# Transposes by the DMA crossbar instead of by TensorE in a sliding-window attention with a two-layer MLP

## The chip, the cores and the metric

The kernel runs on one core of a Trainium2 chip. The metric is the device time of one execution in microseconds (us). The profiler's span, from the first to the last instruction, is 1.7 to 1.9 us shorter than the device time of the same run. Engines are named as the profile names them: PE is TensorE (matmuls), PEld its weight loads, DVE is VectorE, ACT is ScalarE, POOL is GpSimd, SP is SyncE and SPq the queue in which SyncE issues DMAs.

## The reference

Attention over 4 batches of 8 heads, 768 positions, head size 64. Each query sees the 128 latest keys and 4 "sink" keys at the start of its sequence. The result, 3072 x 512, goes through a GEMM to 2048, an exact GELU and a GEMM back to 512.

```python
scores = scale * np.matmul(q, k.transpose(0, 1, 3, 2))
keep = is_sink | in_window            # 4 sinks, window 128
a = softmax(np.where(keep, scores, -1e9))
x = (a @ v).transpose(0, 2, 1, 3).reshape(B * S, H * D)
h = x @ w_in                          # 512 -> 2048
out = (0.5 * h * (1.0 + erf(h * inv_sqrt2))) @ w_out
```

## The kernel before

Queries are worked in 12 groups of 256 (g = 0 to 11), three to a batch, and two groups make a chunk (c = 0 to 5). For each chunk the kernel does the first GEMM (64 matmuls) and then the second (64 matmuls, in 16 slots of 4), and between the matmuls it prepares the attention of the next chunk. During the first GEMM it casts and transposes q and k of the next chunk; in the slots of the second it does scores, exponentials, the product with v (`av`) and the transposes of the result x. So the first GEMM of a chunk needs `xt` complete, which the slots before it produce.

All SyncE DMAs go through one queue, in program order. Loads use a ring of 10 staging tiles; `pump` issues every load whose staging tile the program has already freed.

```python
def casts(g, engs=(nc.vector, nc.vector, nc.vector)):
    for kind, eng in zip("qkv", engs):
        take(kind, g, eng)            # cast, marks the staging tile as free
    pump()                            # issues loads on nc.sync

def qk_transpose(g, pp, eng=nc.vector):
    pt = psB.tile([P, 2, 2, 2, P], BF16, name="qkps", tag="bank")
    # ... eight nc.tensor.transpose into pt
    copy(eng, qkt, pt)
    # ... for groups that begin a batch: 4 small GpSimd copies into SK (sink keys)

def x_transpose(g, p):                # one slot after av(g, p)
    # ... two nc.tensor.transpose into the bank of av
    nc.vector.tensor_copy(out=XT[c][:, p, o : o + Q2], in_=tp)

for c in range(NCH):
    side = {0: lambda: casts(ga), 1: lambda: qk_transpose(ga, 0), 2: lambda: qk_transpose(ga, 1),
            4: lambda: casts(gb), 5: lambda: qk_transpose(gb, 0), 6: lambda: qk_transpose(gb, 1)}
    for f2 in range(NFT // 2):
        gemm1(c, f2)
        if f2 in side:
            side[f2]()
    if c == 0:
        for j in range(8):
            take("wo", j, G_)         # casts of the second weight, on GpSimd
            pump()                    # ... and behind each, a load
    att = attention_slots(c + 1, 16) if nxt else [[] for _ in range(16)]
    for s in range(16):
        gemm2(c, s // 4, s % 4)
        for w in att[s]:
            w()
```

The softmax here doesn't subtract the row's maximum and nothing guards it: scores larger than these inputs give would overflow.

## Time and profile before

| | before |
|---|---|
| device time, median of 4 runs | 264.16 us |
| span of the profiled run | 261.3 us |
| PE busy | 88% of the span |
| DVE, ACT, POOL busy | 47%, 44%, 12% |
| first GEMM of chunk 0 begins | 31.8 us |
| length of chunks 0, 1, 2, 3, 4 | 42.9, 39.4, 38.5, 37.8, 39.4 us |
| chunk 5 and the end | 31.4 us |

Here and below a chunk lasts from the first matmul of its first GEMM to that of the next chunk, read from the order of time on PE. In chunks 1 to 4 PE is nearly always busy. Chunk 0 is longer: PE waits 3.3 us in it for casts of the second weight, which is still being loaded, and its granted clock stood at half until 35.0 us.

### The profile page before, as it was taken

What the parts mean: (1) busy time and instruction counts of PE and PEld (TensorE: products, weight loads), DVE (VectorE), ACT (ScalarE), POOL (GpSimd) and SP (SyncE); (2) the same over time, 40 slices, a digit from 0 to 9 for tenths busy, and PEclk for the clock granted to TensorE, in tenths of its full rate; (3) what the DMA queues carried; (4) which work ended last, traced back from release to release, by engine and by line L of the source; (5) the groups of instructions that cost most, each with busy time, mean ns of one, the idle gap of its engine ahead of it and who ended that gap; (6) DMA issues with size and microseconds to landing.
All of it is one profiled execution on the core that took longest, in us unless ns stands there. A gap on an engine that the chain in (4) does not pass through costs nothing.

```text
span 261.3 us, 4320 instructions
## 1 busy us (share of the span) xinstructions
PE 230.7 (88%) x1734; PEld 118.2 (45%) x1764; DVE 122.1 (47%) x277; ACT 115.4 (44%) x120; POOL 32.4 (12%) x82
## 2 busy tenths in 40 slices
PE   0467699869999989999999999999999989999994
PEld 0235445325445535444535444545445445544441
DVE  0284844247844256844346734357643267610111
ACT  0556336555315585314575325585135666136300
POOL 7177500690000000002000000200000000000000
PEclk9998589999999999999999999999999999999999
DMA  8999999999999991129920146001210010110022
GB/s 155 218 273 348 257 229 271 387 240 229 200 221 283 228 168 43 43 96 225 203 48 34 43 129 112 3 2 41 80 40 3 0 40 4 75 48 0 0 83 80
DMA packets 84756, 33.84 MB, mean 129 GB/s; under 512 B 75520, under 2 KB 79616, under 8 KB 84736
## 3 DMA queue, kind: packets, MB, share of 16 engines
q1 hardware_dynamic: 82656, 33.04, 54.8%
q10 hardware_dynamic: 2080, 0.52, 1.1%
q8 instruction: 14, 0.23, 0.4%
q14 instruction: 6, 0.05, 0.1%
HBM read 27.26 MB, written 6.29 MB: 128 GB/s over the span
## 4 chain that ended last, share of the span: by engine, by line
PE 58%; DMA 13%; DVE 8%; SPq 7%; ACT 7%; issue 5%; POOL 1%; another core or an unknown queue 0%; ACTq 0%; POOLq 0%; DVEq 0%
PE big L399 26%; PE po L418 21%; SPq L170 7%; ACT et L304 5%; DMA st<-in_moe_w_out_dram 5%; DMA st<-in_moe_w_in_dram 4%; DMA st<-in_v_dram 4%; PE qkps L244 3%; DVE osb L427 3%; PE big L295 2%; PE bank L383 2%; DVE x L368 1%; DVE et L315 1%; PE bank L356 1%; ACT gt L407 1%
## 5 line engine op out<-in xcount | busy, mean ns | idle before, releaser
L418 PE MATMUL po<-WOUT,gt 128*128 128x512 bf16 x365 | 91.5, 380 | 5.3 <-POOL WOUT L193 3.3
L399 PE MATMUL big<-xt,WIN 128*128 128x512 bf16 x373 | 88.0, 383 | 0.7 <-issue 0.2
L407 ACT ACTIVATE gt<-big 128x1024 bf16<-128x1024 f32 x48 | 49.1, 1023 | 88.4 <-PE big L399 87.2
L399 PEld LDWEIGHTS <-WIN 128*128 128x128 bf16 x384 | 37.0, 99 | 41.6 <-issue 2.4
L304 ACT ACTIVATE et<-big 128x1024 bf16<-128x1024 f32 (+1 forms) x48 | 44.5, 954 | 19.8 <-PE big L295 11.5
L418 PEld LDWEIGHTS <-gt 128*128 128x128 bf16 x384 | 33.1, 98 | 41.2 <-issue 10.9
L308 DVE TENSOR_TENSOR et<-et,mask 128x1024 bf16<-128x1024 bf16 x32 | 24.2, 758 | 28.7 <-ACT et L304 28.6
L427 DVE COPY osb<-po 128x512 f32<-128x512 f32 x24 | 16.5, 688 | 39.7 <-PE po L418 39.6
L193 DVE COPY qkt<-qkps 128x1024 bf16<-128x1024 bf16 x22 | 15.2, 691 | 35.3 <-PE qkps L244 35.3
L256 POOL COPY sk<-qkt 64x4 bf16<-64x4 bf16 x32 | 6.9, 215 | 129.0 <-DVE qkt L193 127.9
L244 PE MATMUL qkps<-ident,q 128*128 128x128 bf16 x96 | 13.2, 234 | 8.1 <-DVE q L193 7.9
L295 PE MATMUL big<-qkt 64*128 64x128 bf16 (+1 forms) x256 | 18.6, 249 | 2.0 <-ACT et L304 2.0
L368 DVE TENSOR_TENSOR x<-bank,rz 128x256 bf16<-128x256 f32 x44 | 18.7, 424 | 1.5
L356 PE MATMUL bank<-vo,et 128*128 128x65 bf16 x176 | 18.7, 198 | 0.2 <-POOL sk L256 0.2
L383 PE MATMUL bank<-ident,x 128*128 128x128 bf16 x88 | 12.9, 230 | 6.0 <-DVE x L368 5.9
L348 PE MATMUL bank<-vo,et 128*128 128x65 bf16 x148 | 17.2, 197 | 0.1
L383 PEld LDWEIGHTS <-x 128*128 128x128 bf16 x96 | 6.6, 101 | 22.5 <-DVE x L368 20.6
L356 PEld LDWEIGHTS <-et 128*128 128x128 bf16 x192 | 15.8, 103 | 2.0 <-issue 0.9
L348 PEld LDWEIGHTS <-et 128*128 128x128 bf16 x160 | 15.0, 103 | 0.9 <-DVE et L308 0.3
L244 PE MATMUL qkps<-ident,k 128*128 128x128 bf16 x96 | 13.2, 233 | 1.9 <-ACT k L191 1.9
L244 PEld LDWEIGHTS <-q 128*128 128x128 bf16 x96 | 8.9, 105 | 13.0 <-DVE q L193 7.9
L389 DVE COPY xt<-bank 128x256 bf16<-128x256 bf16 x44 | 12.5, 285 | 3.8 <-PE bank L383 3.8
(52 smaller groups left out, 146.5 us busy)
## 6 DMA issues: line engine op xcount, KB each, us to landing
st<-in_q_dram SPq DMA_DIRECT2D x24, 256.0 KB, 5.1
st<-in_v_dram SPq DMA_DIRECT2D x24, 256.0 KB, 4.9
out_dram<-osb SPq DMA_DIRECT2D x24, 256.0 KB, 2.0
st<-in_k_dram SPq DMA_DIRECT2D x22, 256.0 KB, 4.8
st<-in_moe_w_in_dram SPq DMA_DIRECT2D x8, 512.0 KB, 7.9
st<-in_moe_w_out_dram SPq DMA_DIRECT2D x8, 512.0 KB, 9.3
st<-in_k_dram ACTq DMA_DIRECT2D x2, 256.0 KB, 5.6
```

The costliest lines, as they stand in the source:

```text
L244: nc.tensor.transpose(pt[:, a, w, e, :], src[:, e, 2 * p : 2 * p + 2, :].rearrange("s h d -> s (h d)"), ident,)
L295: nc.tensor.matmul(ps[:, hl, c : c + n * P], lhsT=kb[r : r + D, :], rhs=qt(g, p)[r : r + D, e : e + n, :].rearrange("p e n -> p (e n)"), s ...
L304: nc.scalar.activation(out=et[:, :, c0:], in_=ps[:, :, c0:], func=AF.Exp, scale=att_scale)
L308: nc.vector.tensor_tensor(out=et.rearrange("p h (e n) -> p (h e) n", e=2), in0=et.rearrange("p h (e n) -> p (h e) n", e=2), in1=mask.unsqu ...
L348: nc.tensor.matmul(pov[:, e, hl, :], lhsT=et[:, hl, 2 * e * P : (2 * e + 1) * P], rhs=low[:, h, :], start=(i == 0), stop=False, skip_group ...
L356: nc.tensor.matmul(pov[:, e, hl, :], lhsT=et[:, hl, (2 * e + 1) * P : (2 * e + 2) * P], rhs=VO[g][:, e, h, :], start=(low is None), stop=True,
L368: nc.vector.tensor_tensor(out=x4, in0=pv4[:, :, 0:D], in1=rz.unsqueeze(2).to_broadcast((P, 4, D)), op=ALU.mult,)
L383: nc.tensor.transpose(tp[:, e * P : (e + 1) * P], x4[:, 2 * e : 2 * e + 2, :].rearrange("p h d -> p (h d)"), ident,)
L399: nc.tensor.matmul(ph[:, a, :], lhsT=WIN[:, t, ts(f, P)], rhs=XT[c][:, t, :], start=(t == 0), stop=(t == NKT - 1),)
L407: nc.scalar.activation(out=gt, in_=ph, func=AF.Gelu)
L418: nc.tensor.matmul(po, lhsT=GT[c, f // 2][:, f % 2, ts(m, P)], rhs=WOUT[:, f, :], start=(f == 0), stop=(f == NFT - 1),)
L427: nc.vector.tensor_copy(out=osb, in_=po)
```

## The change

The intent is to free PE, the bound, of 240 transposes (and DVE of their copies) by letting the DMA crossbar do them between two places in SBUF, where the DMA engines have time. Groups 0 and 1 stay on PE.

```diff
+    def sink_keys(g):
+        b = g // NBP
+        for h in range(H):
+            p, r = h // 2, D * (h % 2)
+            nc.gpsimd.tensor_copy(out=SK[b % 2][r : r + D, p, h * NS : (h + 1) * NS],
+                                  in_=QKT[g][r : r + D, 1, p, 0, 0:NS])
+    def qk_dma(g):
+        qkt = qk_tile(g)
+        for w, kind in enumerate("qk"):
+            src = cast[kind, g]
+            for e in range(2):
+                nc.sync.dma_start(out=qkt[:, w, :, e, :],
+                                  in_=src[:, e, :, :].rearrange("s h d -> s (h d)"),
+                                  transpose=True)
+        if g % NBP == 0:
+            sink_keys(g)
 ...
     # in av(g, p), for g >= 2, after the last pair of heads
+            for e in range(2):
+                nc.sync.dma_start(out=xt[:, :, o + e * P : o + (e + 1) * P],
+                                  in_=x16[:, e, :, :].rearrange("q h d -> q (h d)"),
+                                  transpose=True)
 ...
-    slots[n + lag_t].append((0, lambda g=g, p=p: x_transpose(g, p)))
 ...
-                0: lambda: casts(ga),
-                1: lambda: qk_transpose(ga, 0),
-                2: lambda: qk_transpose(ga, 1),
-                4: lambda: casts(gb),
-                5: lambda: qk_transpose(gb, 0),
-                6: lambda: qk_transpose(gb, 1),
+                0: lambda: (casts(ga), qk_dma(ga)),
+                3: lambda: (casts(gb), qk_dma(gb)),
```

More of the change, by code (lines that the diff above doesn't have):

```diff
@@ L58 @@
     c16p = ctx.enter_context(tc.tile_pool(name="c16p", bufs=2))
-    qktp = ctx.enter_context(tc.tile_pool(name="qktp", bufs=10))
+    qktp = ctx.enter_context(tc.tile_pool(name="qktp", bufs=4))
     etp = ctx.enter_context(tc.tile_pool(name="etp", bufs=8))
     sink = ctx.enter_context(tc.tile_pool(name="sink", bufs=2))
+    xg = ctx.enter_context(tc.tile_pool(name="xg", bufs=2))
     xp = ctx.enter_context(tc.tile_pool(name="xp", bufs=4))
@@ L233, in sink_values, with qk_tile @@
         )
+    def sink_keys(g):
+        b = g // NBP
+        for h in range(H):
+            p, r = h // 2, D * (h % 2)
+            nc.gpsimd.tensor_copy(
+                out=SK[b % 2][r : r + D, p, h * NS : (h + 1) * NS],
+                in_=QKT[g][r : r + D, 1, p, 0, 0:NS],
+            )
+    def qk_tile(g):
+        if g not in QKT:
+            QKT[g] = qktp.tile([P, 2, NPAIR, 2, P], BF16, name="qkt")
+        return QKT[g]
     def qk_transpose(g, pp, eng=nc.vector):
-        b, i = divmod(g, NBP)
+        qkt = qk_tile(g)
         q16, k16 = cast["q", g], cast["k", g]
         pt = psB.tile([P, 2, 2, 2, P], BF16, name="qkps", tag="bank")
-        for a in range(2):
-            p = 2 * pp + a
-            for w, src in enumerate((q16, k16)):
+        for w, src in enumerate((q16, k16)):
+            for a in range(2):
+                p = 2 * pp + a
                 for e in range(2):
                     nc.tensor.transpose(
-                        pt[:, a, w, e, :],
+                        pt[:, w, a, e, :],
                         src[:, e, 2 * p : 2 * p + 2, :].rearrange("s h d -> s (h d)"),
@@ L248, in qk_transpose @@
                     )
-        qkt = qktp.tile([P, 2, 2, 2, P], BF16, name="qkt")
-        copy(eng, qkt, pt)
-        QKT[g, pp] = qkt
-        if i == 0:
-            for a in range(2):
-                for hl in range(2):
-                    h = 2 * (2 * pp + a) + hl
-                    nc.gpsimd.tensor_copy(
-                        out=SK[b % 2][D * hl : D * hl + D, 2 * pp + a, h * NS : (h + 1) * NS],
-                        in_=qkt[D * hl : D * hl + D, a, 1, 0, 0:NS],
-                    )
+        copy(eng, qkt[:, :, 2 * pp : 2 * pp + 2, :, :], pt)
+    def qk_dma(g):
+        qkt = qk_tile(g)
+        for w, kind in enumerate("qk"):
+            src = cast[kind, g]
+            for e in range(2):
+                nc.sync.dma_start(
+                    out=qkt[:, w, :, e, :],
+                    in_=src[:, e, :, :].rearrange("s h d -> s (h d)"),
+                    transpose=True,
+                )
+        if g % NBP == 0:
+            sink_keys(g)
     def qt(g, p):
-        return QKT[g, p // 2][:, p % 2, 0, :, :]
+        return QKT[g][:, 0, p, :, :]
     def kt(g, p):
-        return QKT[g, p // 2][:, p % 2, 1, :, :]
+        return QKT[g][:, 1, p, :, :]
     ETS = {}
@@ L323, with xt_tile @@
     PO = {}
+    XG = {}
+    def xt_tile(c):
+        if c not in XT:
+            XT[c] = xtp.tile([P, NPAIR, 2 * Q2], BF16, name="xt")
+        return XT[c]
     def av(g, p):
@@ L364, in av @@
         rz = xp.tile([P, 4], FP32, name="rz")
-        x4 = xp.tile([P, 4, D], BF16, name="x4")
+        if g < 2:
+            x4 = xp.tile([P, 4, D], BF16, name="x4")
+            xdst = x4.rearrange("p (e h) d -> p e h d", e=2)
+        else:
+            if p == 0:
+                XG[g] = xg.tile([P, 2, H, D], BF16, name="xg")
+            x4 = None
+            xdst = XG[g][:, :, 2 * p : 2 * p + 2, :]
         pv4 = po[:, 0 : 2 * PV].rearrange("p (n c) -> p n c", c=DV)
@@ L368, in av @@
         nc.vector.tensor_tensor(
-            out=x4,
-            in0=pv4[:, :, 0:D],
-            in1=rz.unsqueeze(2).to_broadcast((P, 4, D)),
+            out=xdst,
+            in0=pov[:, :, :, 0:D],
+            in1=rz.rearrange("p (e h) -> p e h", e=2).unsqueeze(3).to_broadcast((P, 2, 2, D)),
             op=ALU.mult,
         )
-        PO[g, p] = (po, x4)
+        if g < 2:
+            PO[g, p] = (po, x4)
+        elif p == NPAIR - 1:
+            c, o = g // 2, (g % 2) * Q2
+            xt = xt_tile(c)
+            x16 = XG.pop(g)
+            for e in range(2):
+                nc.sync.dma_start(
+                    out=xt[:, :, o + e * P : o + (e + 1) * P],
+                    in_=x16[:, e, :, :].rearrange("q h d -> q (h d)"),
+                    transpose=True,
+                )
     def x_transpose(g, p):
         po, x4 = PO.pop((g, p))
-        c = g // 2
-        if c not in XT:
-            XT[c] = xtp.tile([P, NPAIR, 2 * Q2], BF16, name="xt")
+        xt = xt_tile(g // 2)
         tp = po[:, 3 * P : 4 * P].bitcast(BF16)
@@ L388, in x_transpose @@
         o = (g % 2) * Q2
-        nc.vector.tensor_copy(out=XT[c][:, p, o : o + Q2], in_=tp)
+        nc.vector.tensor_copy(out=xt[:, p, o : o + Q2], in_=tp)
     GT = {}
@@ L436, in units, with attention_slots @@
         return [(g, p) for g in (2 * c, 2 * c + 1) for p in range(NPAIR)]
-    def attention_slots(c, nslots, lag_av=3, lag_t=4):
+    def attention_slots(c, nslots, lag_av=3):
         slots = [[] for _ in range(nslots)]
         for n, (g, p) in enumerate(units(c)):
-            slots[n + lag_t].append((0, lambda g=g, p=p: x_transpose(g, p)))
             slots[n + lag_av].append((1, lambda g=g, p=p: av(g, p)))
@@ L458 @@
     qk_transpose(0, 1, A_)
+    sink_keys(0)
     scores(0, 0)
@@ L512 @@
             if gs:
-                side[3 if gs[0] == ga else 7] = lambda b=gs[0] // NBP: sink_values(b)
+                side[5] = lambda b=gs[0] // NBP: sink_values(b)
         for f2 in range(NFT // 2):
```

## The prediction

> **What bounds the kernel now.** I read the page first, then the busy time by stage, then the order of time on TensorE (PE) and on the DMA-issuing queue of SyncE (SPq). The page:
>
> ```profile
> PE 230.7 (88%) x1734; PEld 118.2 (45%) x1764; DVE 122.1 (47%) x277; ACT 115.4 (44%) x120; POOL 32.4 (12%) x82
> DMA  8999999999999991129920146001210010110022
> L244 PE MATMUL qkps<-ident,q 128*128 128x128 bf16 x96 | 13.2, 234 | 8.1 <-DVE q L193 7.9
> L244 PE MATMUL qkps<-ident,k 128*128 128x128 bf16 x96 | 13.2, 233 | 1.9 <-ACT k L191 1.9
> L383 PE MATMUL bank<-ident,x 128*128 128x128 bf16 x88 | 12.9, 230 | 6.0 <-DVE x L368 5.9
> ```
>
> PE is the bound (88%, next 47%), but the DMA row is at nine tenths for its first 15 slices of 6.5 us, to about 95 us. So there are two halves: until then the loads matter, afterwards PE alone. The busy time by stage (columns: stretch, length, then busy time of each engine, clock, DMA share, GB/s) says the same, second GEMM of chunk 0 against that of chunk 3:
>
> ```profile
> 50.20:74.90 24.70, 21.32 (x185) 10.67 (x189) 14.10 (x36) 10.27 (x12) 8.02 (x10) 1.00 1.07 237
> 168.70:190.50 21.80, 20.71 (x186) 10.45 (x189) 13.31 (x36) 10.94 (x12) 0.00 (x0) 1.00 0.09 37
> ```
>
> What a transpose really takes of PE is its pitch, not its 234 ns, because matmuls overlap. In order of time, first GEMM of chunk 3:
>
> ```profile
> 158.31 0.27 PE L244 MATMUL qkps<-ident,q 128*128 128x128 bf16 x2
> 158.43 0.28 PE L244 MATMUL qkps<-ident,k 128*128 128x128 bf16 x2
> 158.54 0.28 PE L244 MATMUL qkps<-ident,q 128*128 128x128 bf16 x2
> 158.65 0.27 PE L244 MATMUL qkps<-ident,k 128*128 128x128 bf16 x2
> 158.76 5.34 PE L399 MATMUL big<-xt,WIN 128*128 128x512 bf16 x24
> ```
>
> Eight transposes take 158.76 - 158.31 = 0.45 us, 56 ns each: 240 removed transposes are 13.4 us of PE, not 56. Last, the issuing queue, which the change loads further:
>
> ```profile
> 45.95 7.01 SPq L170 DMA_DIRECT2D st<-in_q_dram  x2
> 53.05 4.55 SPq L170 DMA_DIRECT2D st<-in_k_dram  x2
> 57.70 2.05 SPq L170 DMA_DIRECT2D st<-in_v_dram  x2
> ...
> 74.50 2.40 SPq L170 DMA_DIRECT2D st<-in_q_dram  x2
> 77.00 3.16 SPq L429 DMA_DIRECT2D out_dram<-osb  x4
> ```
> ```profile
> 66.01 0.68 DVE L427 COPY osb<-po 128x512 f32<-128x512 f32 x1
> ```
>
> The first output tile is ready at 66.7 us, but the queue comes to it at 77.0. It is in order, and it is stuck behind the eight load tiles (v4 to q7) that the program places ahead of chunk 0's second GEMM. From 59.84 to 77.0 it issues 14 loads in 17.2 us, 1.23 us each; with the rings idle, at 154.21, two loads issue in 1.15. So the rings push back: DMA throughput, some 256 KB / 1.15 us = 228 GB/s. That lateness costs nothing now, since nobody waits for an output.
>
> **What the Trainium skill says.** "VectorE: DVE Perf Modes", The three transpose paths: a 128x128 bf16 transpose is 390 ns on TensorE and 1309 ns through the DMA crossbar. The trace disagrees on the first (219 ns a record, 56 ns pitch) and has no crossbar transpose. "DMA: Bandwidth & Descriptors", Latency and other measured facts: a DMA transpose reached 261 GB/s in one kernel; not shown here either. Same page, Issuing engines are not separate DMA queues: all issuing queues end on the same 16 engines; the backlog above agrees for one queue. "TensorE: Matmul & The Clock Gate", Why this matters for your kernels: PE gaps over about 3 us between matmul bursts bring the half clock back; the trace has the granted clock at 1.00 from 50 us on, with no such gap.
>
> **The change part by part.**
>
> Queries and keys, removed. 32 transposes a chunk (16 for each of its two groups) in chunks 0 to 4: 4 blocks x 0.45 = 1.8 us of the PE path per chunk. In chunk 0 the second GEMM waits for its weights anyway (PE waits for the WOUT casts), so I count 4 x 1.8 = 7.2 us. The DVE copies of qkt (20 x 0.69 = 13.8 us) go too, but DVE is no bound: nothing.
>
> Attention output, removed. 16 transposes a chunk, 0.9 us, for five chunks. With them go PE's waits for DVE's x, since each slot began with the transpose of what DVE had just finished: 0.7 to 1.1 us a chunk in the waits by stage, and as the modelled matmul ends hide about 0.17 us at each of two, 1.2. Together 2.1 us a chunk, 10.5 us in all. The PSUM bank is also free earlier, so no bank wait should replace it. Best case: 7.2 + 10.5 = 17.7 us, or 246.5 us.
>
> Added: 12 DMAs of 128x512 bf16 (128 KB) a chunk on the same queue, 8 for q and k and 4 for x. At 261 GB/s one is 0.50 us of the rings. For the path between issues I take 1.3 us each, reading the page's 1309 ns as the fixed part of one DMA rather than as a rate. Both are estimates from those pages. Per steady chunk the queue then has 12 x 1.3 = 15.6 us of transposes plus at most 12 loads x 0.8 = 9.6 and 4 outputs x 0.33 = 1.3: 26.5 of some 36 us. It fits, but it has an order.
>
> - Chunk 0, the new wait. The order becomes: wo6, transposes of group 2, wo7, q4, k4, transposes of group 3, the eight load tiles, and only then the x transposes that the first GEMM of chunk 1 needs. The last weight load takes 12.31 us to land in the chain (44.69 to 57), so group 2's transposes land near 57 and group 3's near 57 + 2 + 4 loads x 1.15 + 2 = 66; PE's slot 4 starts there and not at 59.4. The queue comes to x at 77.0 + 8 x 0.5 = 81.0. Four transposes (5.2) with two outputs (0.6) end at 86.8, and some 1.7 us to land gives 88.5. The first GEMM of chunk 1 starts there and not at 74.7: +14 us.
> - That idle stretch may cool PE's clock: +1.5 us.
> - Each later chunk boundary (1 to 4). After the last av, 20 matmuls remain before the next first GEMM (0.216 each, 4.3 us). DVE needs 0.9 us for its x, two issues 2.6, landing some 2: 5.5. So 1.2 us of stall, 4.8 in all.
> - Group b's q and k in chunks 1 and 2, behind 12 loads: 9.6 + 10.4 + 2 = 22 us after the chunk begins, needed at 13.8 + 4 slots x 1.6 = 20.2. The casts can run a little ahead of PE: 0.5 us each, 1.0.
>
> Chunks 1 to 4 gain 4 x (1.8 + 2.1) = 15.6, lose 5.8: -9.8. Chunk 0 with its boundary: +14 + 1.5, in which its own gain of 2.1 is already swallowed. Sum +5.7 us, 264.2 + 5.7 = 269.9; I say 269.
>
> **The rivals.**
>
> 1. All hidden: PE gets the 17.7 us, or 14 with short boundary waits: 247 to 252 us. For it: the rings are at 0.05 to 0.41 of their time in the second GEMMs from 91 us on. Against it: the queue's ten-microsecond lag at 77.0, seen above. It needs the x transposes not to be behind the loads, and they are.
> 2. The page's 1309 ns is a rate: 128x512 is four of them, 5.2 us a DMA. 12 x 5.2 = 63 us a chunk against 36: the crossbar becomes the bound, five chunks x 63 + 75 = about 390 us. For it: nothing in the trace; against it, 261 GB/s on the other page. Even at 2.5 us a DMA it is about 300. This is the long upper tail.
> 3. Small in the balance: transposes near 0.5 us also in issue, so x lands near 80 and the later boundaries do not stall: +6 - 15.6 + 2 = -8, 256 us.
> 4. DVE freed of 24 us brings the time down: no, at 47% it sets the end nowhere except in x before the x transpose, counted above.
>
> **Range and chances.** The one large term, +14, has a spread of about 8 us either way (transposes of 0.5 to 2 us; how far the backlog lasts), the gains about 4, the boundaries about 4. So 256 to 287, longer above because of rival 2. The borders of 2% are 258.9 and 269.5. Faster 0.17, within 0.33, slower 0.50.
>
> **What would show it.** After: no L244 or L383 transposes on PE past chunk 0's start, some 13 us fewer PE pitches; a gap on PE of ten or more microseconds ahead of the first GEMM of chunk 1, ended by the DMA into xt; the x transposes issued near 81 to 87 us, right behind the load of q7; sink scores of group 2 waiting to about 57; gaps near 1 us at later boundaries, likewise ended by xt; chunks 3 and 4 shorter by 2 to 3 us than before. I am wrong if PE goes on at 75 to 78 us (the order did not matter), if a transpose holds the rings over 2 us (rival 2), or if scores, not xt, are what PE waits for in later chunks.

## The result

The changed kernel takes 278.6 us (278.49 to 278.69, 4 runs) against 264.16 us: slower by 5.5%, ratio 1.0550 with a 95% interval of 1.0532 to 1.0568. A ratio here is the mean time of one kernel's runs over that of the other's in the same rounds, so it is not quite the ratio of the medians. The results agree with the reference. The direction was the likeliest one of the prediction and the time lies in its range, but the loss is 14.4 us where 4.8 was forecast: wrong by a factor of three.

The page of the changed kernel (busy time by engine; then the busy tenths of PE, its clock and the DMA engines in 40 slices of 6.9 us; then the shares of the chain that ended last; then two groups with idle time and releaser):

```profile
PE 223.8 (81%) x1498; PEld 109.1 (39%) x1524; DVE 99.9 (36%) x217; ACT 115.6 (42%) x120; POOL 30.9 (11%) x82
PE   0477799001999499999999499999999999999994
PEclk9998599855799779999999959999999999999999
DMA  8999999994999798925799903693034500230011
PE 52%; SPq 18%; DMA 16%; DVE 5%; issue 4%; ACT 3%; POOL 2%; DVEq 0%; ACTq 0%; POOLq 0%
L459 PE MATMUL po<-WOUT,gt 128*128 128x512 bf16 x366 | 93.3, 390 | 21.5 <-POOL WOUT L194 19.4
L440 PE MATMUL big<-xt,WIN 128*128 128x512 bf16 x376 | 88.5, 393 | 5.5 <-DMA xt<-xg 4.8
```

PE's share fell from 88% to 81% with some holes: slices 7 to 9 (48 to 68 us) are all but empty, and two later slices stand at 4. The issuing queue SPq has 18% of the chain, 7% before. Chunk by chunk (differences from the unrounded starts):

| | before | after | difference |
|---|---|---|---|
| chunk 0 | 42.9 | 62.7 | +19.8 |
| chunk 1 | 39.4 | 38.6 | -0.9 |
| chunk 2 | 38.5 | 41.9 | +3.4 |
| chunk 3 | 37.8 | 34.3 | -3.5 |
| chunk 4 | 39.4 | 35.7 | -3.8 |
| ahead of and behind these | 63.2 | 63.6 | +0.4 |

So chunks 3 and 4 are what was hoped for, and the loss is in chunks 0 and 2. In order of time, PE in chunk 0 of the changed kernel (start, length, instruction; in brackets the idle time before it and what ended that):

```profile
45.17 3.63 PE L440 MATMUL big<-xt,WIN 128*128 128x512 bf16 x15
68.16 2.00 PE L459 MATMUL po<-WOUT,gt 128*128 128x512 bf16 x4 [19.37 <-POOL WOUT L194]
...
94.60 16.84 PE L440 MATMUL big<-xt,WIN 128*128 128x512 bf16 x63 [4.03 <-DMA xt<-xg]
```

And GpSimd in the same stretch:

```profile
65.27 1.74 POOL L240 COPY sk<-qkt 64x4 bf16<-64x4 bf16 x8 [33.52 <-DMA qkt<-k]
67.07 8.40 POOL L194 CAST WOUT<-st 128x1024 bf16<-128x1024 f32 x8
```

PE waits 19.4 us for a cast of the second weight. GpSimd could have done that cast long before (at 45.6 us in experiment 1), but it works in order, and ahead of the casts stand the eight copies of group 3's sink keys, which wait for the crossbar. I had not looked at GpSimd at all. The issuing queue:

```profile
45.26 5.41 SPq L272 DMA_TRANSPOSE qkt<-q  x2
50.72 3.62 SPq L272 DMA_TRANSPOSE qkt<-k  x2
...
59.57 3.12 SPq L272 DMA_TRANSPOSE qkt<-q  x2
62.74 2.57 SPq L272 DMA_TRANSPOSE qkt<-k  x2
68.14 0.99 SPq L171 DMA_DIRECT2D st<-in_v_dram  x2
...
83.51 2.88 SPq L171 DMA_DIRECT2D st<-in_q_dram  x2
86.49 0.95 SPq L470 DMA_DIRECT2D out_dram<-osb  x1
87.54 2.54 SPq L413 DMA_TRANSPOSE xt<-xg  x2
```

The x transposes do stand right behind the load of q7, as predicted, but at 87.5 us rather than 81. Chunk 2 has another wait, for q and k of its second group:

```profile
157.45 0.60 PE L292 MATMUL bank<-qkt,sk 128*128 128x256 bf16 x4 [3.10 <-DMA qkt<-q]
...
159.46 0.29 PE L314 MATMUL big<-qkt 64*128 64x128 bf16 x2 [1.08 <-DMA qkt<-k]
```

Two explanations of chunk 0 are possible. Theory G: GpSimd's wait is the cause; take it away and the 19 us come back. Theory Q: the x transposes are behind the loads in the queue; take GpSimd's wait away and PE will only wait later, for xt.

### The profile page after: what moved, and what is told of

The parts are those of the page before. It is cut to its first block, busy times and chain, and to the rows that moved or that the text cites. A ratio compares the mean times of both kernels' runs of the same rounds, so it can differ in the third digit from the quotient of the medians.

```text
span 276.8 us, 3890 instructions
## 1 busy us (share of the span) xinstructions
PE 223.8 (81%) x1498; PEld 109.1 (39%) x1524; DVE 99.9 (36%) x217; ACT 115.6 (42%) x120; POOL 30.9 (11%) x82
## 4 chain that ended last, share of the span: by engine, by line
PE 52%; SPq 18%; DMA 16%; DVE 5%; issue 4%; ACT 3%; POOL 2%; DVEq 0%; ACTq 0%; POOLq 0%
PE po L459 22%; PE big L440 21%; SPq L171 9%; SPq L272 7%; DMA xt<-xg 5%; PE big L314 4%; DMA st<-in_v_dram 4%; DMA st<-in_moe_w_in_dram 4%; DMA qkt<-k 3%; DVE osb L468 2%; PE bank L381 2%; ACT et L323 1%; PE bank L373 1%; PE bank L361 1%; PE bank L292 1%
## 5 line engine op out<-in xcount | busy, mean ns | idle before, releaser
L459 PE MATMUL po<-WOUT,gt 128*128 128x512 bf16 x366 | 93.3, 390 | 21.5 <-POOL WOUT L194 19.4
L440 PEld LDWEIGHTS <-WIN 128*128 128x128 bf16 x384 | 38.1, 101 | 55.4 <-issue 14.3
L400 DVE TENSOR_TENSOR xg<-bank,rz 128x256 bf16<-128x256 f32 x40 | 17.0, 424 | 1.4
L300 ACT ACTIVATE ets<-bank 128x256 bf16<-128x256 f32 x8 | 3.1, 384 | 26.8 <-PE bank L292 26.8
L314 PEld LDWEIGHTS <-qkt 64*128 64x128 bf16 x256 | 8.2, 98 | 12.9 <-issue 8.5
L334 DVE TENSOR_TENSOR et<-et,mask 128x768 bf16<-128x768 bf16 x16 | 8.9, 556 | 10.9 <-ACT et L323 10.4
L361 PE MATMUL bank<-vsk,ets 128*128 128x130 bf16 x60 | 12.3, 224 | 0.1
L194 DVE CAST q<-st 128x1024 bf16<-128x1024 f32 x12 | 8.2, 687 | 8.1 <-DMA st<-in_q_dram 8.1
L292 PE MATMUL bank<-qkt,sk 128*128 128x256 bf16 x32 | 5.7, 300 | 4.4 <-DMA qkt<-q 3.1
L399 DVE RECIPROCAL rz<-bank 128x4 f32<-128x4 f32 x44 | 7.8, 177 | 3.9 <-PE bank L381 3.6
```

The lines of the kernel that those rows point to most:

```text
L314: nc.tensor.matmul(ps[:, hl, c : c + n * P], lhsT=kb[r : r + D, :], rhs=qt(g, p)[r : r + D, e : e + n, :].rearrange("p e n -> p (e n)"), s ...
L400: nc.vector.tensor_tensor(out=xdst, in0=pov[:, :, :, 0:D], in1=rz.rearrange("p (e h) -> p e h", e=2).unsqueeze(3).to_broadcast((P, 2, 2, D ...
L440: nc.tensor.matmul(ph[:, a, :], lhsT=WIN[:, t, ts(f, P)], rhs=XT[c][:, t, :], start=(t == 0), stop=(t == NKT - 1),)
L459: nc.tensor.matmul(po, lhsT=GT[c, f // 2][:, f % 2, ts(m, P)], rhs=WOUT[:, f, :], start=(f == 0), stop=(f == NFT - 1),)
```

## The experiments

Nine kernels ran; all were correct. In each heading stand the median and the ratio to the kernel before, from runs on the same chip.

### 1. Sink keys after the weight casts: 275.9 us, 1.0453 (1.0415 to 1.0491)

```diff
-        if g % NBP == 0:
+        if g % NBP == 0 and g != 3:
             sink_keys(g)
 ...
         for j in range(8):
             take("wo", j, G_)
             pump()
+        sink_keys(3)
```

> One call moved: in chunk 0 the eight GpSimd copies of group 3's sink keys come after the eight casts of the second weight, not before. Theory G (GpSimd, in order, held the weight casts behind a copy that waits for the crossbar: 48.4 to 68.2 us of idle TensorE): the second GEMM of chunk 0 starts near 50 to 58 us and all of it comes off, about -14 us or more, 262 to 265 us. Theory Q (the one on record: the x transposes sit behind the loads in the issuing queue): TensorE starts early but then waits for xt, because the loads v4 to q7 still issue after group 3's transposes (65.3 us instead of 68.1) for some 18.6 us; xt lands near 91.8 instead of 94.6, so only -3 us, 274 to 276 us, with the idle stretch moved from before the second GEMM to after it.

PE's waits in chunk 0 in order of time, then the queue, of this kernel:

```profile
56.02 1.01 PE L292 MATMUL bank<-qkt,sk 128*128 128x256 bf16 x4 [6.20 <-DMA qkt<-q]
...
65.68 0.28 PE L314 MATMUL big<-qkt 64*128 64x256 bf16 x2 [1.69 <-DMA qkt<-k]
...
91.99 3.57 PE L440 MATMUL big<-xt,WIN 128*128 128x512 bf16 x8 [12.53 <-DMA xt<-xg]
```
```profile
83.74 1.09 SPq L470 DMA_DIRECT2D out_dram<-osb  x1
84.92 2.54 SPq L413 DMA_TRANSPOSE xt<-xg  x2
```

Theory G falls, theory Q holds. The second GEMM of chunk 0 now begins at 48.8 us instead of 68.2, yet chunk 1 begins at 91.99 us (91.8 was expected). The longest wait of the whole profile, 19.4 us, was worth 62.7 - 60.9 = 1.8 us of chunk 0; a wait of 12.5 us for xt and others for q and k stand where it was. These are the prediction's own waits, at their times: the sink scores of group 2 at 56.0 us (57 forecast) and the scores of group 3 at 65.7 (66). What it did cost is that GpSimd's late casts also kept staging tiles from the loads, so that v4 was issued at 68.1 us rather than 65.8. (One profile of each kernel: chunk 0 begins between 30.9 and 32.3 us in kernels whose program is the same up to there, so terms of chunk 0 are known to about 1 us.)

### 2. Transposes ahead of the loads: 268.0 us, 1.0160 (1.0135 to 1.0186)

```diff
     def casts(g, ...):
         for kind, eng in zip("qkv", engs):
             take(kind, g, eng)
-        pump()
 ...
-                0: lambda: (casts(ga), qk_dma(ga)),
-                3: lambda: (casts(gb), qk_dma(gb)),
+                0: lambda: (casts(ga), qk_dma(ga), pump()),
+                3: lambda: (casts(gb), qk_dma(gb), pump()),
```

> In every chunk the q and k transposes are issued ahead of the loads that the same casts set free, not behind them. Theory G and Q together: in chunk 0 the transposes land some 5 to 10 us earlier, the copies of the sink keys and so the weight casts too, but the last weight tile lands later and the x transposes still follow the same loads: chunk 0 shorter by 2 to 5 us at most. Chunk 2, where sink scores and scores waited 4.2 us for q and k of group 7 and the clock fell: the wait goes, -6 us. Sum 267 to 272 us. If the q and k wait in chunk 2 were not from the queue's order but from the crossbar's own rate, chunk 2 stays at about 42 us and the sum is 275 or more.

Chunk 0 60.9 us (1.8 less), chunk 1 37.9, chunk 2 34.7: 7.3 us less, and no wait for qkt is left in it. So chunk 2's loss was the order of the queue. Of the 7.3 us, 3.10 + 1.08 are the wait itself; the rest goes with the clock, which fell after it. The busy time by stage of the changed kernel (stretch, length, busy time of PE, PEld, DVE, ACT, POOL, then granted clock, DMA share, GB/s):

```profile
154.00:159.50 5.50, 1.32 (x17) 0.78 (x15) 1.36 (x4) 0.44 (x2) 0.00 (x0) 0.91 0.89 167
159.50:166.80 7.30, 6.97 (x53) 3.42 (x54) 3.17 (x7) 3.07 (x3) 0.00 (x0) 0.60 0.11 33
```

After the stretch in which PE was busy for only 1.32 of 5.5 us, it worked at a granted clock of 0.60 for about 7 us.

### 3. Queries and keys of chunk 1 on PE: 267.7 us, 1.0152 (1.0113 to 1.0191)

```diff
+            if c == 0:
+                side = {
+                    0: lambda: (casts(ga), pump()),
+                    1: lambda: qk_transpose(ga, 0),
+                    2: lambda: qk_transpose(ga, 1),
+                    4: lambda: (casts(gb), pump()),
+                    5: lambda: qk_transpose(gb, 0),
+                    6: lambda: (qk_transpose(gb, 1), sink_keys(gb)),
+                }
```

> Queries and keys of groups 2 and 3 on TensorE as before, all else as in the changed kernel, so chunk 0 keeps only its x transposes on the crossbar. Theory Q: the queue comes to them at 77 us as it came to the outputs in the kernel before; two outputs and four transposes of 1.25 us and 2.5 us to land make xt complete near 85, so chunk 1 begins at 84 to 86 us instead of 94.6, and with the clock kept up somewhat the time is 264 to 268 us. Theory G alone (the x transposes are hidden once GpSimd isn't held): chunk 1 begins at 75 to 77 us and the time is 255 to 259 us.

The queue of this kernel:

```profile
73.82 2.42 SPq L171 DMA_DIRECT2D st<-in_q_dram  x2
76.34 1.09 SPq L470 DMA_DIRECT2D out_dram<-osb  x1
77.52 2.61 SPq L413 DMA_TRANSPOSE xt<-xg  x2
```

It comes to the first output at 76.3 us, as the kernel before did (77.0), and with the x transposes behind it chunk 1 begins at 84.66 us. Theory Q expected 84 to 86. Chunk 0 lasts 53.5 us: its x transposes alone, behind the loads, cost 53.5 - 42.9 = 10.6 us. With experiment 1 the rest follows: the eight q and k transposes cost 60.9 - 53.5 = 7.4 us, which is also the lag of the first output in the queue, 83.74 - 76.34.

### 4. All transposes of groups 2 and 3 on PE: 263.5 us, 0.9986 (0.9957 to 1.0014)

As experiment 3, and:

```diff
-        if g < 2:            # x on PE (two places)
+        if g < 4:
 ...
+            if g < 4:
+                slots[n + 4].append((0, lambda g=g, p=p: x_transpose(g, p)))
```

> The change from the third chunk on: all transposes of groups 2 and 3, queries, keys and outputs, on TensorE, the crossbar for groups 4 to 11. Chunk 0 then is that of the kernel before (42.9 us). Chunks 3 and 4 gain 3.5 and 3.9 us as in the changed kernel. Chunk 1: the queue is behind there (loads to 93 us in the kernel before), so group 4's transposes follow loads and land near 93 and group 5's near 106, against needs of 88 and 100: it loses up to 5 us net or gains 3.9 if the queue keeps up. Chunk 2 between +3.5 and -3.9. So 253 to 262 us, best guess 258. If the steady gain were an artefact of the late start of chunk 1 (more slack for loads), chunks 3 and 4 gain less than 2 us each and the time is 262 or more.

My best guess, 258 us, was missed, and so was the range. Chunk 0 is back at 43.2 us and chunks 3 and 4 keep their gain (34.2 and 35.6 us), so the gain is no artefact of a late start. But chunk 1 takes 44.0 us, 4.6 more than before, and chunk 2 40.9: with PE early again, q and k of groups 4 and 5 are late too, behind their loads (waits for qkt of 5.0 us in chunk 1 and 4.4 in chunk 2). The changed kernel's chunk 1 had been spared this only because it began some 19 us later (94.6 us against 75.4).

### 5. Experiments 2 and 4 together: 250.3 us, 0.9515 (0.9477 to 0.9553)

> The two edits that helped, together: groups 2 and 3 wholly on TensorE, and from group 4 on the q and k transposes issued ahead of the loads. If the queue's order is all that kept the crossbar from paying, chunk 0 stays at 43.2 us, chunk 1 falls from 44.0 to about 35.7, chunk 2 from 40.9 to 34.7, chunks 3 and 4 stay at 34.3 and 35.7: span near 247 us, time 248 to 251 us, faster than both kernels by 5%. If the crossbar beside running loads is slow of itself (rings shared), chunk 1 stays above 38 us and the time above 253.

The chunks last 43.6, 37.3, 34.8, 34.2 and 35.6 us. The time is as expected and beats both kernels. One of its six runs took 253.16 us; it is in the mean. The queue in chunk 1 shows why the order suffices (it is still late, with outputs at 76.3 us, but q and k are now next):

```profile
76.31 2.67 SPq L469 DMA_DIRECT2D out_dram<-osb  x4
79.08 3.99 SPq L271 DMA_TRANSPOSE qkt<-q  x2
...
85.75 1.20 SPq L171 DMA_DIRECT2D st<-in_k_dram  x2
```

### 6. Everything on the crossbar, half of the loads behind x: 264.0 us, 1.0015 (0.9985 to 1.0045)

As experiment 2, and:

```diff
         for j in range(8):
             take("wo", j, G_)
-            pump()
+            pump(34)                 # only v4, q5, k5, v5
+        sink_keys(3)
 ...
         for s in range(16):
             gemm2(c, s // 4, s % 4)
             for w in att[s]:
                 w()
+            if c == 0 and s == 10:
+                pump()               # the rest, after group 3's x
```

> All groups from the second chunk on stay on the crossbar, as in the changed kernel with the transposes first, but two orders are changed in chunk 0: sink keys of group 3 after the weight casts, and of the eight load tiles in front of the x transposes only four stay there, the other four being issued after the transposes of group 3's x. Theory Q: the queue comes to x some 9.4 us earlier, xt is complete near 82 instead of 91.8 us; some of it is given back in chunk 1, where the four deferred tiles stand before q and k (up to 6 us). 256 to 263 us against 268.0 without these edits. If the order of the queue is not what holds chunk 1's begin, it stays at 90 us or later and the time at 267 or more.

The queue comes to x at 76.6 us instead of 84.7, and chunk 1 begins at 84.1 instead of 91.8 (82 was expected), so the order of the queue is what holds it. Chunk 1 gives 4.9 us back (42.8 against 37.9), waiting for q and k behind the four deferred tiles, as feared. The time is 1 us above the range. The two edits were made together, so their shares aren't separated here.

### 7. Experiment 5 with merged transposes: 247.5 us, 0.9390 (0.9366 to 0.9415)

```diff
-            for e in range(2):
-                nc.sync.dma_start(out=qkt[:, w, :, e, :], in_=src[:, e, :, :]..., transpose=True)
+            nc.sync.dma_start(out=qkt[:, w, :, :, :].rearrange("f e p n -> f (e p) n"),
+                              in_=src.rearrange("s e h d -> s (e h d)"), transpose=True)
```

(The same for x. The transposed tiles are laid out with the half e ahead of the pair p, so that the two halves are one run of blocks.)

> As the kernel with groups 2 and 3 on TensorE and transposes first, but with one transpose DMA of 128 by 1024 for two of 128 by 512 (six a chunk, not twelve; the layouts of the transposed tiles are changed to fit). If the 1.25 us in which the queue is held is a fixed part of each DMA, the queue is held about 1.3 us for twice the data, and what waits remain at chunk boundaries shrink: time equal or up to 1.5 us less. If the hold goes with size, each takes 2.5 us and the time stays within 1 us or is a little more. The rows of TensorE read with a stride; if that cost anything the GEMM stages would be longer than 13.8 us.

The queue's issues of x, of experiment 5 and of this one (count, then minimum, median and maximum in ns of the hold, the time for which one issue occupies the queue, then first and last start):

```profile
L412 SPq DMA_TRANSPOSE xt<-xg x16: 1189/1256/1799, 105.0 to 214.1; - x16
```
```profile
L414 SPq DMA_TRANSPOSE xt<-xg x8: 1237/1242/1879, 102.2 to 211.1; - x8
```

Twice the data holds the queue no longer where nothing is backed up ahead of it: the hold is fixed there, 1.24 us. Landing takes a median of 3.1 us instead of 2.5. The gain, 2.8 us, is larger than I expected, 2.0 of it in chunk 1 (35.3 us). The GEMMs read xt with a stride now and still take 13.8 us in chunk 1: no cost is seen. This is the fastest kernel.

### 8. Only x through the crossbar: 256.9 us, 0.9746 (0.9723 to 0.9769)

As experiment 5, but the q and k transposes on PE in every chunk.

> As the kernel with groups 2 and 3 on TensorE, but queries and keys on TensorE in all chunks; only the attention output of groups 4 to 11 goes through the crossbar. If the two parts add up: the first GEMM of chunks 1 to 4 takes 15.6 to 16.0 us as in the kernel before (1.8 more than without transposes), the second GEMM stages keep their 1.7 to 1.9 us of gain: 264 minus 4 x 1.8 gives 256 to 258 us. If the output's part had been paid for with waits for xt at the boundaries, it would be 260 or more.

As expected. The first GEMMs of chunks 1 to 4 take 15.6 to 16.0 us (13.8 to 14.3 in experiment 5), the second ones 20.0 to 22.4. The two halves of the change add up: q and k are worth 1.8 us a chunk, x 1.4 to 2.1 in its own place.

### 9. The changed kernel with merged transposes: 269.1 us, 1.0222 (1.0169 to 1.0275)

The edit of experiment 7 on the changed kernel itself, with its orders.

> The changed kernel as it is, orders and all, but with one transpose DMA of 128 by 1024 in place of two of 128 by 512. In the runs so far the merged DMA held the queue 1.24 us, as long as one of half the size, while its share of the 16 engines' time stayed at some 0.7 to 0.8 us per 128 KB. If in chunk 0, where the engines are full, it is the engines' time that the eight q and k transposes cost (7.4 us), chunk 0 stays within 1.5 us of 62.7 us; only chunk 2, where the queue's own time made q and k of group 7 late, loses its wait and the slow clock after it (41.9 to about 35 us): 269 to 272 us in all. If it is the hold of 1.25 us each, chunk 0 shortens by some 4 us as well: 264 to 268 us.

The time is as expected. Chunk 0 stays at 62.1 us and chunk 2 falls from 41.9 to 35.9. So in chunk 2 fewer holds all but remove the wait for q and k (0.4 us is left) that experiment 2 removed by the order. In chunk 0, where the DMA engines are full, merging did not take the hold away. The queue of this kernel:

```profile
44.73 6.46 SPq L275 DMA_TRANSPOSE qkt<-q  x1
51.24 3.51 SPq L275 DMA_TRANSPOSE qkt<-k  x1
...
60.24 2.33 SPq L275 DMA_TRANSPOSE qkt<-q  x1
62.61 1.31 SPq L275 DMA_TRANSPOSE qkt<-k  x1
```

Four issues held it 13.6 us; the eight of the changed kernel, shown above, 14.7. That fits a cost set by the engines' time there, but does not show it: the wait for GpSimd, 19.6 us here, is in this chunk too. The queue entry of the kernel before and of the changed kernel (packets, MB, share of 16 engines) gives an estimate of that time:

```profile
q1 hardware_dynamic: 82656, 33.04, 54.8%
```
```profile
q1 hardware_dynamic: 115296, 40.91, 69.4%
```

0.694 x 276.8 - 0.548 x 261.3 = 48.9 us for 60 transposes, 0.81 us each, if the other DMAs' packets took as long in both. Where no load runs beside them, from 210.6 to 222.5 us of the changed kernel, the packets of eight transposes took 5.25 us of the engines: 0.66 us each, some 200 GB/s. The loads of q, k and v move in packets of the same 256 bytes, at 182 GB/s in the kernel before. Eight transposes are 5.3 to 6.5 us by these two measures, most of the 7.4 that they cost in chunk 0.

Part of chunk 1's fall in this run, to 35.3 us, is a warmer clock: its first GEMM took 13.8 us against 16.7.

```profile
94.39 13.97 PE L444 MATMUL big<-xt,WIN 128*128 128x512 bf16 x64 [2.80 <-DMA xt<-xg]
```

PE had waited 2.8 us for xt here, 4.0 in the changed kernel.

## Why the prediction was right or wrong

The sum was +5.7 us; the span grew by 15.5. Term by term:

| term of the prediction | predicted | measured |
|---|---|---|
| chunk 0, x behind the loads, without the q and k transposes ahead | +9.8 (14 - 4.0 - 0.2) | +10.6 (experiment 3) |
| chunk 0, q and k transposes ahead of it, "8 x 0.5" | +4.0 | +7.4 (experiments 1, 3) |
| chunk 0, GpSimd held by sink keys | not seen | +1.8 (experiment 1) |
| the clock after the idle stretch | +1.5 | +2.9 (first GEMM of chunk 1, after 4.0 us of waiting for xt) |
| group b's q and k, chunks 1 and 2 | +1.0 | +7.3, all in chunk 2 (experiment 2) |
| stalls at the boundaries of chunks 1 to 4 | +4.8 | under 1 |
| PE's gain, chunks 1 to 4 | -15.6 | -14.9 |
| ahead of chunk 0 and behind chunk 4 | 0 | +0.4 |

(The 0.2 is rounding: 77.0 + 5.8 + 1.7 - 74.7 = 9.8. The measured gain, in which the small boundary stalls are contained, is -3.5 and -3.8 in chunks 3 and 4; chunk 1 without the 2.9 us of clock gives -3.7, and chunk 2 without its wait, from experiment 2, -3.9. The measured column sums to 15.5, as the spans differ.)

The step that failed most is the term for group b's q and k: 6.3 of the 9.8 us by which the sum fell short. The q and k transposes of chunk 0 add 3.4, GpSimd 1.8 and the clock 1.4; boundaries and gains together erred by 4.1 the other way.

**Right: what PE gains.** 56 ns of pitch a transpose, 1.8 us per chunk for q and k, 1.4 to 2.1 for x and its wait: shown in chunks 3 and 4 and in experiment 8. Of the wait for DVE only 0.3 us are left, in chunk 4. **Right: the mechanism of chunk 0.** The queue comes to x only behind the load of q7. The gap of ten or more us ahead of chunk 1 that I named as its sign is not in the changed kernel, which waits only 4.0 us there, since GpSimd's wait hides the rest; experiment 1 shows it, 12.5 us. The sign of rival 1's failure, the ten-microsecond lag of an output that nobody waited for, was the right thing to read in the profile before.

**Wrong: "The queue comes to x at 77.0 + 8 x 0.5 = 81.0."** It came to the first output at 86.5 and to x at 87.5. The 0.50 us was 128 KB at the 261 GB/s of the Trainium skill ("DMA: Bandwidth & Descriptors", Latency and other measured facts); here a transpose took 0.66 us of the engines alone, 0.81 by the estimate over the whole run, and the eight made the queue 7.4 us later. The small rest was GpSimd: for the second GEMM I foresaw waits for transposed q and k, to about 57 and 66, and for its weights no more than before. I had followed PE's consumers of the transposed keys, but not GpSimd's, nor what stands behind those on GpSimd.

**Wrong: "Group b's q and k ... 0.5 us each."** I had 22 us after the chunk's begin against a need at 20.2, and took most of the difference off because casts can run ahead. In chunk 2 the last transpose of group 7 was issued from 156.9 us and the scores that needed it ran at 159.5, 26.3 us after the chunk's begin at 133.2. The loads ahead took 1.0 us each where I had 0.8 (12.3 us for twelve, not 9.6), the eight transposes 11.2 us, not 10.4, and a wait of 4.2 us brought 3 us of slow clock with it. Chunk 1 escaped by its late start, as experiment 4 shows.

**Wrong, in the other direction: 1.2 us at each boundary.** At the begin of chunk 4 PE waited 0.26 us for xt. The second x transpose is issued 1.25 us after the first and lands 2.5 us after that issue begins; I had 2.6 us for two issues and another 2 to land.

Rival 2, 1309 ns as a rate, is refuted: twice the data takes the same hold. Rival 1's time is reached once the order of the queue is right, experiment 5 at 250.3 us lying in its 247 to 252, but with groups 2 and 3 left on PE. With groups 2 to 11 all on the crossbar no kernel's median came below 264.0 us (experiment 6).

One reading in the working is wrong: 1.15 us is the time of two loads at idle rings, and the backlog's own 1.23 us a load is 213 GB/s, not 228. It does not enter the sum.

Open: how much of chunk 0's 7.4 us is the engines' time of the transposes (5.3 to 6.5 us) and how much the holds, which lasted 1.3 to 2.9 us there, was not separated further; experiment 9 only says that halving their number changed chunk 0 by 0.6 us and their sum by 1.1. A second issuing queue for the loads or the outputs was not tried.

## What to carry to other kernels

A DMA moved onto the critical path inherits everything ahead of it in its queue: look in the profile before for transfers that are issued late and that nobody waits for, because the lateness is invisible until someone does. Ask the same of every in-order engine that reads what you are delaying, and of what stands behind that reader. And don't take the longest wait at its length: the wait of 19.4 us was worth 1.8, because another wait, for the same queue, ended almost as late.

## What the Trainium skill lacked or had wrong

- "VectorE: DVE Perf Modes", The three transpose paths, has 1309 ns for a 128x128 crossbar transpose and does not say what that time is. Here the issuing queue was held 1.24 to 1.26 us (medians) by a transpose of 128x512 and 1.24 us by one of 128x1024, and the data landed 2.5 and 3.1 us after the issue began. The hold is fixed at these sizes, so merging pays. Behind a backlog of loads the hold grew to 2.95 us, and to 6.46 us for a merged one (experiment 9).
- The same section has 390 ns for TensorE and does not say there that in a stream the pitch is what counts: it was 56 ns, and that is what a removed transpose gave back. (The pitch of a stream of matmuls does stand elsewhere in the skill.)
- "DMA: Bandwidth & Descriptors", Latency and other measured facts, has 261 GB/s for a transpose with a middle dimension that isn't contiguous. From SBUF to SBUF in 128x512 bf16 pieces it was some 200 GB/s of engine time with no load beside it, and 161 by the estimate over the whole run. That transposes are as fast as regular DMAs, as "Advanced Engine Details and Errata", X-Bar Transpose (TRN2), says, agrees with the loads that move in packets of the same 256 bytes, 182 GB/s.
- "DMA: Bandwidth & Descriptors", Issuing engines are not separate DMA queues, calls the time to initiate a DMA usually small relative to the DMA. For these transposes the hold, 1.25 us, is longer than their 0.66 to 0.81 us of engine time, and the order in one queue cost 10.6 us in chunk 0 and 7.3 us in chunk 2.
- "TensorE: Matmul & The Clock Gate", Why this matters for your kernels, warns of gaps over about 3 us between bursts of matmuls. Single gaps agree: after 4.0 us of waiting for xt the first GEMM of chunk 1 took 16.7 us, after 2.8 us (experiment 9) 13.8. But several shorter ones did it too. In chunk 1 of experiment 4 no wait was longer than 1.7 us, PE was busy for 2.9 us of 5.0, and the granted clock of the next 3.4 us was 0.51.
